# Sparse attention and two feed-forward layers on one core: a four-byte constant is allocated in front of x^T

## The chip, the core and the metric

The kernel runs on 1 core of one Trainium2 chip. Its measure is the device time of one execution in microseconds: the median of three runs of the kernel before is 643.96 us (643.88 to 644.82).

The engines carry these names in the profile: PE is TensorE's matmul row, PEld its weight loads, DVE is VectorE, ACT is ScalarE, POOL is GpSimd, and SP issues the DMAs. A matmul has two operands in SBUF: the *stationary* one, which a weight load brings into the array, and the *moving* one, whose columns stream through it.

## The reference

Attention with 8 global columns and a causal band of 96, a linear distance bias for each head, softmax, and then two feed-forward layers on the 1536 tokens of 512 features:

```python
def _attn_ref(q, k, v, n_global, n_local):        # q, k, v: (2, 8, 768, 64)
    scores = scale * np.matmul(q, k.transpose(0, 1, 3, 2)) + bias
    scores = np.where(keep, scores, -1000000000.0)
    a = softmax(scores)
    return np.matmul(a, v)

def _moe_ref(x, w_in, w_out):                     # layer 0; d_ff = 2048
    h = x @ w_in
    g = np.maximum(h, 0.0) + np.log1p(np.exp(-np.abs(h)))
    return g @ w_out

def _moe2_ref(x, w_in, w_out):                    # layer 1
    h = x @ w_in
    g = h * np.clip(h + 3.0, 0.0, 6.0) / 6.0
    return g @ w_out
```

The weights arrive as 64-bit floats.

## The kernel before

**Two paths.** `fast_path` does the work for the usual counts of global and local columns. `general_path` stands behind a branch that is not taken with these inputs, so none of it is in the profile.

**Numbers as pairs.** Each 32-bit operand is kept as a high and a low part in the matmul type (names ending in h and l: `xsh`/`xsl` are x^T, `gh`/`gl` the activations of a layer). A product is three matmuls (`matmul3`, L193): low times high, high times low, high times high, all added up in PSUM. Nearly all of TensorE's work is recorded at L193.

**Weights.** SyncE loads a block of 64-bit words (`raw`, L114), and ScalarE, GpSimd and VectorE rebuild from it the two parts (L133 to L146; `wa` is the value in between). A chunk of 128 hidden features has four tiles `w`. There are 11 slots of such tiles for the 32 chunks of both layers; a slot is freed when the last group of tokens has used its chunk.

**Stages.** In the first (to about 208 us) the attention of the blocks of 128 tokens runs between the first chunks of layer 0, in matmuls of 256 columns: `hf` is x times w_in, `accf` the product with w_out. From there on `item` works on 512 tokens and one chunk at a time, in matmuls of 512 columns: 12 for `h` and 12 for `acc`. `h` has a weight tile as stationary and x^T as moving operand. `acc` of layer 0 has the weight tile as stationary and the activation as moving operand, and `acc` of layer 1 the other way round. Sums over chunks that don't fit in PSUM at a time go to the tiles `part` (L289, L295, L297).

**The last group.** `last_items` computes `h` of five chunks (`hz` in the profile) and then all of their second products in one go (`accz`, to the end of the kernel). Its activations don't lie in the pool of `gh` and `gl`; they are put into weight slots that have become free:

```python
            wp, t = self.free.pop(0)
            where = [wp.tile([P, CW], F32R, tag=f"w{i}_{t}", name=f"g{i}_{s}") for i in range(2)]
            g.append(self.split_g(1, h, f"z{s}", where))
```

**A check of the inputs** runs beside layer 1: 24 loads of blocks of q and k (`chk`, L623) whose squares ScalarE sums (L624); they use the buffers of `raw`.

**Order.** A list scheduler of the framework sets the order on each engine when the kernel is built; on the chip each engine works its list off in that order.

**The constant.** `three` holds 3.0 in one 4-byte column, which layer 1's activation takes as its bias (L182). `Layers` allocates it in the pool `pp`, behind the three tiles `part`, and fills it on VectorE (L67):

```python
        self.three = self.pp.tile([P, 1], F32, name="three")
        self.nc.vector.memset(self.three, 3.0)
```

Of the kernel before, what the change touches and what calls it, by code (L numbers as in the profile page):

```python
# [7 lines left out]
F32 = mybir.dt.float32  # L8
# [8 lines left out]
P = 128  # L17
# [34 lines left out]
class Layers:  # L52
# [3 lines left out]

    def __init__(self, ctx, tc, weights, xsh, xsl, out):
        self.ctx, self.tc, self.nc = ctx, tc, tc.nc  # L60
        self.weights, self.xsh, self.xsl, self.out = weights, xsh, xsl, out
        self.pool("mp", 2)
        self.pool("tp", 5)
        self.pool("pp", 1)
        self.part = [self.pp.tile([P, 4, GB], F32, name=f"part{g}") for g in range(T // GB)]
        self.three = self.pp.tile([P, 1], F32, name="three")
        self.nc.vector.memset(self.three, 3.0)  # L67
        self.W, self.raws, self.slot = {}, {}, {}
        self.done, self.loaded = 0, 0
        first = range(PHASES[0][0])  # L70
        early = range(2 * EARLY_PAIRS)
        self.order = [(j, u) for js in (early, first[len(early):]) for u in range(2) for j in js]
        self.order += [(j, u) for j in range(len(first), 2 * NCH) for u in range(2)]
        self.free, self.h_tags, self.acc_tags, self.wr = [], [], [], []
        self.room = None
        self.n_h, self.halves, self.in_first, self.beside = 0, 0, True, False
        self.grow(0, FIRST_SLOTS, 2, 2)
# [318 lines left out]
def x_tiles(ctx, tc):  # L396
    xp = ctx.enter_context(tc.tile_pool(name="xp", bufs=1))
    return tuple(
        [xp.tile([P, KC, GB], F32R, name=f"xs{z}{g}") for g in range(T // GB)] for z in "hl"
    )  # L400
# [7 lines left out]
        nc.gpsimd.tensor_scalar(out=t, in0=t, scalar1=rs[:, j:j + 1], scalar2=0.0, op0=ALU.mult, op1=ALU.add)  # L408


def fast_path(tc, ident, nf, counts, q, k, qt, kt, v, weights, out, flag):


    with ExitStack() as ctx, ExitStack() as actx:
        nc = tc.nc
        xsh, xsl = x_tiles(ctx, tc)
        layers = Layers(ctx, tc, weights, xsh, xsl, out)
        layers.beside = True
        tp = layers.tp
        layers.room = actx.enter_context(tc.tile_pool(name="ap_r", bufs=1))  # L420
# [330 lines left out]
                    nc.vector.tensor_tensor(out=xl, in0=px, in1=r32(xh), op=ALU.subtract)  # L751


def general_path(tc, ident, nf, q, k, v, weights, out):
    with ExitStack() as ctx:
        xsh, xsl = x_tiles(ctx, tc)
        dense_attention(tc, ident, nf, q, k, v, xsh, xsl)
        layers = Layers(ctx, tc, weights, xsh, xsl, out)
        layers.weight_step(2 * FIRST_SLOTS)
        layers.run()  # L760


def body(tc, q, k, v, qt, kt, ns, w1i, w1o, w2i, w2o, out):
    nc = tc.nc
    with ExitStack() as ctx:
        nc.scalar.preload_act_table_set("natural_log_exp_and_others")
        const = ctx.enter_context(tc.tile_pool(name="const", bufs=1))
        ident = const.tile([P, P], F32, name="ident")

        nsb = const.tile([P, 2, 2], I32, name="nsb")  # L770
        nc.sync.dma_start(out=nsb.rearrange("p n w -> p (n w)"), in_=ns.partition_broadcast(P))
        nf = const.tile([P, 2], F32, name="nf")
        cv = const.tile([P, 2, 2], F32, name="cv")
        cneg = const.tile([P, 2], F32, name="cneg")

        def counts():
            tc.keep_in_program_order(nc.vector.tensor_copy(cv, nsb))
            nc.vector.tensor_scalar(out=cneg, in0=cv[:, :, 0], scalar1=0.0, scalar2=None, op0=ALU.is_lt)
            nc.vector.tensor_tensor(out=cneg, in0=cneg, in1=cv[:, :, 1], op=ALU.add)
            nc.vector.scalar_tensor_tensor(  # L780
                out=nf, in0=cneg, scalar=float(2 ** 32), in1=cv[:, :, 0], op0=ALU.mult, op1=ALU.add
            )

        make_identity(nc, ident)
        flag = const.tile([1, 1], I32, name="flag")
        weights = (w1i, w1o, w2i, w2o)
        fast_path(tc, ident, nf, counts, q, k, qt, kt, v, weights, out, flag)
        redo = nc.values_load(flag[0:1, 0:1], min_val=0, max_val=1)
        with tc.If(redo > 0):
            general_path(tc, ident, nf, q, k, v, weights, out)  # L790


def layout(q, k, v, n_global, n_local, moe_w_in, moe_w_out, moe2_w_in, moe2_w_out):
# [43 lines left out]
```

## Time and profile before

| | us |
|---|---|
| median of three runs | 643.96 (643.88 to 644.82) |
| the profiled execution | 643.55 |
| its span, first to last instruction | 641.8 |

The profile is of one execution. Besides the busy time of each engine it gives the chain of work that ended last (each piece is what released the next one), what each engine waited for, and the granted clock of TensorE. A matmul's own duration says little about TensorE's pace, since matmuls follow each other into the array before the one ahead has left it; the pace is the time from one start to the next. It is read from a run of n matmuls in the chain (the time that the piece covers, by n), or from a row of the timeline, which covers the first start to the last end: that time less one matmul's duration, by n - 1.

### The profile page before, as it was taken

The page shows a single profiled execution, that of the slowest core. Times are in us where ns is not written, and L with a number is a line of the kernel's source. Part 1 is how long each engine was busy: PE and PEld are TensorE (multiplying, and loading weights), DVE is VectorE, ACT ScalarE, POOL GpSimd, SP SyncE. Part 2 cuts the span into 40 slices and gives each one's busy share as a digit, 9 for nine tenths or more (in the row PEclk, how much of TensorE's full clock was granted, in tenths as well). Part 3 has the DMA queues.
Part 4 walks back from the last instruction along what each step waited for, and adds up shares of the span by engine and source line. Part 5 has one row for each costly group of instructions (what it writes and reads, how often), then busy time and mean ns, then how long its engine had stood idle before and what let it go on. Part 6 is the DMA issues. An engine that isn't in the chain of part 4 may idle for free.

```text
span 641.8 us, 9651 instructions
## 1 busy us (share of the span) xinstructions
PE 622.3 (97%) x3496; PEld 513.1 (80%) x3496; DVE 425.7 (66%) x893; ACT 380.8 (59%) x808; POOL 148.1 (23%) x180
## 2 busy tenths in 40 slices
PE   8699999999999999999999999999999999999996
PEld 4477987899999888887888888888887888888785
DVE  6988687735799999999989994126723342424251
ACT  7978888764868877696777652326694222222230
POOL 4666354330133255352200600001000000000000
PEclk9989999999999999999999999999999999999999
DMA  8754231101233333433402132001562000001011
GB/s 279 247 172 137 72 100 38 42 5 66 73 126 133 130 115 118 131 130 100 132 1 66 66 106 91 0 1 33 164 197 67 0 1 0 2 1 65 1 67 70
DMA packets 25081, 53.67 MB, mean 84 GB/s; under 512 B 2496, under 2 KB 9152, under 8 KB 25024
## 3 DMA queue, kind: packets, MB, share of 16 engines
q1 hardware_dynamic: 25024, 52.96, 25.4%
q8 instruction: 29, 0.48, 0.3%
q14 instruction: 28, 0.23, 0.1%
HBM read 49.81 MB, written 3.15 MB: 83 GB/s over the span
## 4 chain that ended last, share of the span: by engine, by line
PE 62%; DVE 17%; ACT 9%; DMA 5%; issue 3%; POOL 3%; SPq 0%; ACTq 0%; POOLq 0%; DVEq 0%
PE acc L193 21%; PE h L193 21%; PE accf L193 6%; PE hf L193 5%; ACT pm L523 3%; DVE wa L140 2%; DMA chk<-in_q 2%; PE accz L193 2%; PE hz L193 2%; DVE wa L141 2%; DVE w L146 2%; PE ptp L546 2%; POOL wa L136 1%; ACT chk L624 1%; PE px L564 1%
## 5 line engine op out<-in xcount | busy, mean ns | idle before, releaser
L193 PE MATMUL h<-xsh,w 128*128 128x512 f32 x584 | 159.1, 396 | 0.0
L136 POOL TENSOR_SCALAR wa<-wa 128x512 f32<-128x512 f32 x56 | 79.4, 1423 | 235.4 <-ACT wa L133 235.2
L193 PEld LDWEIGHTS h<-xsh,w 128*128 128x128 f32 x584 | 109.3, 188 | 26.7 <-DVE t L179 0.7
L193 PE MATMUL acc<-w,gh 128*128 128x512 f32 x344 | 108.0, 395 | 0.0
L183 DVE SCALAR_TENSOR_TENSOR t<-t,h 128x512 f32<-128x512 f32 x43 | 29.4, 684 | 82.3 <-ACT t L182 82.3
L193 PE MATMUL h<-xsl,w 128*128 128x512 f32 x292 | 82.3, 395 | 0.0
L182 ACT ACTIVATE t<-h,three 128x512 f32<-128x512 f32 x43 | 29.5, 687 | 87.7 <-PE h L193 87.5
L185 DVE TENSOR_TENSOR gl<-t,gh 128x512 fp32r<-128x512 f32 x73 | 51.3, 703 | 42.9 <-ACT gh L184 42.6
L193 PE MATMUL acc<-gh,w 128*128 128x512 f32 x240 | 78.9, 396 | 0.3 <-DVE part L289 0.2
L193 PEld LDWEIGHTS acc<-w,gh 128*128 128x128 f32 x344 | 64.5, 188 | 15.7
L184 ACT CAST gh<-t 128x512 fp32r<-128x512 f32 x73 | 45.2, 619 | 46.3 <-PE acc L193 24.3
L193 PE MATMUL acc<-w,gl 128*128 128x512 f32 x172 | 68.2, 396 | 0.1
L408 POOL TENSOR_SCALAR pm<-pm,rs 128x256 f32<-128x256 f32 (+1 forms) x96 | 54.4, 585 | 58.9 <-DVE rs L406 34.2
L193 PEld LDWEIGHTS h<-xsl,w 128*128 128x128 f32 x292 | 54.8, 188 | 13.2
L193 PE MATMUL accf<-ghf,w 128*128 128x256 f32 x288 | 56.6, 286 | 0.2 <-ACT ghf L184 0.2
L193 PEld LDWEIGHTS acc<-gh,w 128*128 128x128 f32 x240 | 44.9, 188 | 11.9 <-DVE part L289 0.6
L523 ACT ACTIVATE pm<-pm,nm 128x256 f32<-128x256 f32 (+1 forms) x96 | 46.3, 485 | 3.3 <-DVE nm L518 3.1
L193 PE MATMUL acc<-gl,w 128*128 128x512 f32 x120 | 47.5, 396 | 0.0
L193 PE MATMUL hf<-xsh,w 128*128 128x256 f32 x288 | 47.2, 289 | 0.0
L193 PEld LDWEIGHTS accf<-ghf,w 128*128 128x128 f32 x288 | 45.9, 188 | 0.6 <-ACT ghf L184 0.4
L146 DVE TENSOR_TENSOR w<-wa,w 128x512 fp32r<-128x512 f32 x56 | 39.4, 705 | 8.9 <-ACT w L145 8.9
L145 ACT CAST w<-wa 128x512 fp32r<-128x512 f32 x56 | 34.3, 615 | 14.4 <-DVE wa L141 8.9
(115 smaller groups left out, 1045.9 us busy)
## 6 DMA issues: line engine op xcount, KB each, us to landing
raw<-in_w2i SPq DMA_DIRECT2D x16, 512.0 KB, 3.3
raw<-in_w2o SPq DMA_DIRECT2D x16, 512.0 KB, 3.3
raw<-in_w1i SPq DMA_DIRECT2D x14, 512.0 KB, 3.4
raw<-in_w1o SPq DMA_DIRECT2D x12, 512.0 KB, 3.3
V<-in_v SPq DMA_DIRECT2D x12, 256.0 KB, 3.0
chk<-in_q SPq DMA_DIRECT2D x12, 256.0 KB, 3.0
chk<-in_k SPq DMA_DIRECT2D x12, 256.0 KB, 2.8
qT<-in_qt SPq DMA_DIRECT2D x11, 256.0 KB, 3.9
```

Source lines behind the costliest of these rows:

```text
L136: nc.gpsimd.tensor_scalar(out=a, in0=a, scalar1=W_HI, scalar2=W_LO, op0=ALU.min, op1=ALU.max)
L140: nc.vector.scalar_tensor_tensor(out=ai, in0=hi, scalar=-2 ** 30, in1=ai, op0=ALU.bitwise_and, op1=ALU.bitwise_or)
L141: nc.vector.scalar_tensor_tensor(out=ai, in0=lo, scalar=29, in1=ai, op0=ALU.logical_shift_right, op1=ALU.bitwise_or)
L145: nc.scalar.copy(wh, a)
L146: nc.vector.tensor_tensor(out=wl, in0=a, in1=r32(wh), op=ALU.subtract)
L182: nc.scalar.activation(t1, hf, AF.Relu, bias=self.three[:, 0:1])
L183: nc.vector.scalar_tensor_tensor(out=t3, in0=t1, scalar=6.0, in1=hf, op0=ALU.min, op1=ALU.mult)
L184: nc.scalar.copy(gh, t3)
L185: nc.vector.tensor_tensor(out=gl, in0=t3, in1=r32(gh), op=ALU.subtract)
L193: return self.nc.tensor.matmul(out, lhsT=a, rhs=b, start=start and z == 0, stop=stop and z == len(seq) - 1, **kw)
L408: nc.gpsimd.tensor_scalar(out=t, in0=t, scalar1=rs[:, j:j + 1], scalar2=0.0, op0=ALU.mult, op1=ALU.add)
L523: nc.scalar.activation(pmz, pmz, AF.Exp, bias=nm[:, z:z + 1], scale=-1.0, accum_out=sm[:, z:z + 1])
```

## The change

`three` is allocated in `body`, as the last tile of the pool `const`, and handed to `Layers`; it is filled there once, instead of once on each path. The pool `const` lies in front of all others, and a tile takes up at least 32 bytes of each partition. So what follows `const` moves up by 32 bytes, up to the place where `three` was: behind that nothing moves, since the 32 bytes there are gone.

```diff
-    def __init__(self, ctx, tc, weights, xsh, xsl, out):
+    def __init__(self, ctx, tc, weights, three, xsh, xsl, out):
...
-        self.three = self.pp.tile([P, 1], F32, name="three")
-        self.nc.vector.memset(self.three, 3.0)
+        self.three = three
...
-        layers = Layers(ctx, tc, weights, xsh, xsl, out)
+        layers = Layers(ctx, tc, weights, three, xsh, xsl, out)
...
         flag = const.tile([1, 1], I32, name="flag")
+        three = const.tile([P, 1], F32, name="three")
+        nc.vector.memset(three, 3.0)
         weights = (w1i, w1o, w2i, w2o)
```

The addresses in the two built programs (bytes from the start of a partition, and modulo 128):

| tiles | before | modulo 128 | after | modulo 128 |
|---|---|---|---|---|
| `three` | 109344 | 32 | 17184 | 32 |
| `xsh0`, the first of the six x^T tiles | 17184 | 32 | 17216 | 64 |
| `gh`, `gl`, all of layer 0 and layer 1 up to the last group | | 32 | | 64 |
| scratch of the activations (`t`) | | 32 | | 64 |
| `part0`, the first of three | 84768 | 32 | 84800 | 64 |
| the first weight tile; all 256 weight tiles and the last group's `g` | 109376 | 64 | 109376 | 64 |
| `raw`, `wa`, `chk`, `kT`, `qT`, `V`, `pm`, `pT` | | 64 | | 64 |

All tiles of x^T, of the activations and of the weights begin at one and the same address modulo 2048: the first two at 800 before and 832 after, the weights at 832 in both. On every engine the instructions of the fast path stand in the same order in both programs, with the same shapes; one VectorE memset of the path that isn't taken is gone.

## Rows read from the trace of the kernel before

**Rows 1.** The page: span, and busy time of each engine with its share.

```profile
span 641.8 us, 9651 instructions
PE 622.3 (97%) x3496; PEld 513.1 (80%) x3496; DVE 425.7 (66%) x893; ACT 380.8 (59%) x808; POOL 148.1 (23%) x180
```

**Rows 2.** Busy time of the engines by stretch; columns in the first row.

```profile
core 0: us, PE busy (x) PEld busy (x) DVE busy (x) ACT busy (x) POOL busy (x), PEclk, DMA share, GB/s
145.83:208.35 62.52, 62.52 (x481) 60.36 (x482) 51.48 (x91) 45.35 (x80) 14.32 (x13) 1.00 0.30 102
208.35:301.45 93.10, 92.78 (x396) 73.92 (x396) 91.81 (x159) 69.94 (x122) 40.15 (x22) 1.00 0.38 124
301.45:444.19 142.74, 142.74 (x611) 114.74 (x612) 98.31 (x163) 80.37 (x136) 19.61 (x14) 1.00 0.17 56
444.19:490.77 46.58, 46.45 (x199) 36.90 (x198) 24.66 (x40) 34.18 (x81) 2.87 (x4) 1.00 0.50 147
490.77:621.49 130.72, 130.72 (x561) 105.19 (x562) 48.22 (x74) 32.04 (x49) 0.00 (x0) 1.00 0.05 17
```

**Rows 3.** Chain of work in order of time: start us, us, what; TensorE's pieces.

```profile
157.38 2.84 PE hf L193 x24
...
205.49 2.85 PE accf L193 x24
...
305.61 2.80 PE acc L193 x12
308.41 2.80 PE h L193 x12
...
508.76 2.80 PE acc L193 x12
```

**Rows 4.** Timeline of TensorE in the last stage: start us, us, what, count.

```profile
622.49 9.23 PE L193 MATMUL accz<-w,g 128*128 128x512 f32 x40
...
631.79 1.48 PE L193 MATMUL accz<-w,g 128*128 128x256 f32 x11
```

**Rows 5.** Groups by line: busy us, mean ns of one, idle before.

```profile
L193 PE MATMUL accz<-w,g 128*128 128x512 f32 x45 | 10.4, 389 | 0.0
...
L193 PE MATMUL hf<-xsl,w 128*128 128x256 f32 x144 | 22.9, 281 | 0.0
L185 DVE TENSOR_TENSOR gl<-t,gh 128x512 fp32r<-128x512 f32 x73 | 51.3, 703 | 42.9 <-ACT gh L184 42.6
L146 DVE TENSOR_TENSOR w<-wa,w 128x512 fp32r<-128x512 f32 x56 | 39.4, 705 | 8.9 <-ACT w L145 8.9
```

**Rows 6.** The chain where TensorE is not on it: start us, us, what.

```profile
249.00 4.37 DMA raw<-in_w2o
...
300.78 0.63 ACT gh L184
...
301.45 1.19 PE acc L193 x4
...
444.21 0.63 ACT w L145
...
452.40 3.18 DMA chk<-in_q
...
490.02 0.70 DVE gl L185
...
490.77 3.07 PE acc L193 x12
```

**Rows 7.** Busy time in 145.83 to 208.35 us: tile `hf`, then tile `accf`.

```profile
145.83:208.35 62.52, 24.05 (x192) 1.00 0.30 102
...
145.83:208.35 62.52, 30.19 (x240) 1.00 0.30 102
```

**Rows 8.** Shares of the chain in 0 to 145.83 us, by line.

```profile
by line: ACT pm L523 12.8%; PE accf L193 8.4%; PE ptp L546 7.7%; PE hf L193 7.6%; PE px L564 5.6%; DVE pm L518 5.3%; PE s L512 4.2%; issue 3.9%; POOL pm L408 3.8%; ACT pT L548 3.6%; DVE part L141 2.8%; DVE w L146 2.8%; DVE part L140 2.4%; D
```

More of the change, by code (lines that the diff above doesn't have):

```diff
@@ L408, in softmax_rows, with fast_path @@
         nc.gpsimd.tensor_scalar(out=t, in0=t, scalar1=rs[:, j:j + 1], scalar2=0.0, op0=ALU.mult, op1=ALU.add)
-def fast_path(tc, ident, nf, counts, q, k, qt, kt, v, weights, out, flag):
+def fast_path(tc, ident, three, nf, counts, q, k, qt, kt, v, weights, out, flag):
     with ExitStack() as ctx, ExitStack() as actx:
@@ L751, in dense_attention, with general_path @@
                     nc.vector.tensor_tensor(out=xl, in0=px, in1=r32(xh), op=ALU.subtract)
-def general_path(tc, ident, nf, q, k, v, weights, out):
+def general_path(tc, ident, three, nf, q, k, v, weights, out):
     with ExitStack() as ctx:
@@ L757, in general_path @@
         dense_attention(tc, ident, nf, q, k, v, xsh, xsl)
-        layers = Layers(ctx, tc, weights, xsh, xsl, out)
+        layers = Layers(ctx, tc, weights, three, xsh, xsl, out)
         layers.weight_step(2 * FIRST_SLOTS)
@@ L785, in body @@
         flag = const.tile([1, 1], I32, name="flag")
+        three = const.tile([P, 1], F32, name="three")
+        nc.vector.memset(three, 3.0)
         weights = (w1i, w1o, w2i, w2o)
-        fast_path(tc, ident, nf, counts, q, k, qt, kt, v, weights, out, flag)
+        fast_path(tc, ident, three, nf, counts, q, k, qt, kt, v, weights, out, flag)
         redo = nc.values_load(flag[0:1, 0:1], min_val=0, max_val=1)
         with tc.If(redo > 0):
-            general_path(tc, ident, nf, q, k, v, weights, out)
+            general_path(tc, ident, three, nf, q, k, v, weights, out)
 def layout(q, k, v, n_global, n_local, moe_w_in, moe_w_out, moe2_w_in, moe2_w_out):
```

## The prediction

> **What bounds the kernel now.** First the busy times [rows 1]: TensorE's matmuls are busy for 97% of the span, its weight loads for 80%, no other engine for more than 66%. That alone doesn't say that its pace sets the end, so next come the busy times by stretch [rows 2], cut where the chain of work changes hands. From 145.83 to 208.35, 301.45 to 444.19 and 490.77 to 621.49 us TensorE is busy all the time at the full granted clock (1.00), and the chain in these stretches is TensorE's own matmuls, one behind the other [rows 3]. In the two stretches between, TensorE is busy nearly all the time too, but the chain runs elsewhere [rows 6]. From 208.35 to 301.45 VectorE is busy for 91.81 of 93.10 us, rebuilding weights and splitting activations, and TensorE has a matmul of `acc` waiting at 301.45 for ScalarE's `gh`. From 444.21 it goes through ScalarE and the loads of the input check, one behind the other; at 490.77 `acc` starts when VectorE's `gl` is ready. There TensorE is not ahead: the others set the time.
>
> So the question is TensorE's pace. In runs of 512 columns it is the same for all three uses: `h`, `acc` of layer 0 and `acc` of layer 1 take 2.80 us for 12, 233.3 ns each [rows 3]. Their operands lie at 64 (the weight) and 32 (x^T or activation) modulo 128, whichever of the two is stationary. One run differs: `accz`, the last group. 40 matmuls of it cover 9.23 us [rows 4]; less one duration of 389 ns [rows 5], by 39, that is 226.7 ns. It has the shape, type, PSUM accumulation and three-part order of `acc`. What it has of its own is where its activations lie: in weight slots, so both operands begin at 64. That is the pair of places that the change gives to every matmul of `h` and `acc`.
>
> In runs of 256 columns the sign is the other way: `hf` takes 2.84 us for 24, 118.3 ns, and `accf` 2.85 [rows 3]; the 256-column end of `accz`, both operands at 64, takes (1.48 - 0.28)/10 = 120.0 ns [rows 4, 5].
>
> [...]
>
> **The change part by part.**
>
> *512 columns.* The pace goes from 233.3 to 226.7 ns, 2.84% of the time that such matmuls set.
> - 301.45 to 444.19: 142.74 us x 2.84% = -4.05.
> - 490.77 to 621.49: 130.72 x 2.84% = -3.71.
> - 145.83 to 208.35: 481 matmuls [rows 2], less 192 `hf` and 240 `accf` [rows 7], leave 49 of 512 columns: 49 x 6.6 ns = -0.32.
> - 208.35 to 301.45: nothing. TensorE reaches each wait sooner and waits longer. If it did set the pace there, this would be -2.64. What hides it is VectorE's list, which is full.
> - 444.21 to 490.77: nothing, by the chain of loads and ScalarE. If that gave way, -1.32. Its start is moved with TensorE: ScalarE's `w` at 444.21 stands right behind `acc`, whose weight slot it writes. So what was won before 444 us isn't lost here.
> - `accz` itself has this pace already.
>
> *256 columns.* +1.7 ns each. In 145.83 to 208.35 us all 432 are on the chain: +0.73. Before that `accf` and `hf` hold 8.4% and 7.6% of 145.83 us of chain [rows 8], 23.3 us or 197 matmuls: +0.33. Together +1.06. Bounds: 0, since interrupted runs may not settle into the slower pace, and 864 x 1.7 ns = +1.47, if all were on the chain.
>
> *Other engines.* VectorE's subtraction takes 703 ns on activations (at 32 before) and 705 on weights (at 64) [rows 5]. Same operation, same shape: the place costs these engines nothing that can be read, and I take 0. The one memset stays first on VectorE, so no wait is added.
>
> *Sum.* -4.05 - 3.71 - 0.32 + 1.06 = -7.02 us. The profiled execution took 643.55 us, 1.75 more than its span of 641.8; it becomes 636.5. The median of 643.96 lies 0.4 above it, and I forecast that: 643.96 - 7.02 = **636.9 us**. Next to be late are the same two chains, which then make TensorE wait about 2.6 and 1.3 us longer.
>
> **The rivals.**
>
> *The two chains give way.* If VectorE's list and the check move up with TensorE, because they wait for its results more than the chain shows, all stretches gain: -7.02 - 2.64 - 1.32 = -10.98, so 633.0, and 631.9 without the 256-column loss. Against it: VectorE is idle for only 1.29 us in 93.10 [rows 2], and the check is a row of loads of about 3 us [rows 6].
>
> *Half of it.* Only one operand's place matters. Then `h`, whose weight is stationary before and after, and `acc` of layer 1 can't both gain: about half of -8.08, plus 1.06, gives -2.98, so 641.0. Against it: `h` and layer 1's `acc` have the pair the opposite way round and the same pace [rows 3].
>
> *No change.* `accz` is quick for another reason, such as the quiet around it, with hardly any work on other engines. Then 644.0. Against it: from 490.77 to 621.49 VectorE is idle for 82 of 130.72 us, and the pace is 233.3 ns there [rows 2, 3]. For it: a single run of 45 matmuls in one place of the program is all the evidence. [...]
>
> *Slower.* Operands that begin at the same place get in each other's way, as the 256-column end of `accz` hints with its +1.7 ns. If the 512 columns pay that too: (142.74 + 130.72)/0.2333 + 49 = 1221 matmuls x 1.7 ns = +2.08, with the +1.06 gives +3.14, so 647.1. It decides once the 512-column pace of `h` comes out above 233.3 ns. Against it: 512-column `accz` went down.
>
> That the addresses don't move is no rival: they are read from the two programs.
>
> **How the numbers follow.** The forecast (636.9; 634.5 to 639.5 with its own bounds) has 0.55, the chains giving way 0.10, half 0.11, no change 0.16, slower 0.08. The range 632.5 to 644.0 holds the forecast, the half, most of the first rival and half of the no-change case, about 0.8. A measurement of this kernel can tell about 0.2%, 1.3 us, from no change. Faster by more: 0.55 + 0.10 + 0.11 = 0.76; within: 0.16; slower: 0.08.
>
> **What would show each step.** Pieces of the chain with 12 `h` or `acc` at 2.72 us instead of 2.80 show the pace; 2.80 shows the no-change case, and a difference between `h` and layer 1's `acc` the half. `hf` at 2.88 for 24 shows the loss at 256 columns. TensorE's idle time in front of `acc` near 300 and 490 us, grown by 2.6 and 1.3 us, shows the two chains holding; no growth shows them giving way. VectorE's `gl` off 703 ns would make the zero for other engines wrong. The forecast as a whole is wrong if the pace of `accz` was not due to its addresses.

## The result

The changed kernel takes 637.11 us (median of four runs, 635.96 to 637.76), the kernel before 643.98 (643.88 to 644.82). The ratio is 0.9882, with a 95% interval of 0.9866 to 0.9898: faster by 6.9 us, where 7.0 was forecast. The profiled execution of the changed kernel is the quickest of its four, 635.96 us with a span of 634.2.

In the changed kernel the line numbers are one less: L192 is what L193 was. First the busy times by stretch, cut where the chain changes hands as in [rows 2] (columns in the first row; the fourth row is the stretch of the check):

```profile
core 0: us, PE busy (x) PEld busy (x) DVE busy (x) ACT busy (x) POOL busy (x), PEclk, DMA share, GB/s
145.83:208.83 63.00, 63.00 (x482) 61.03 (x482) 52.14 (x91) 45.24 (x80) 12.63 (x13) 1.00 0.31 101
208.83:302.12 93.29, 91.21 (x397) 73.54 (x396) 92.16 (x158) 70.27 (x122) 34.46 (x22) 1.00 0.38 124
302.12:440.88 138.76, 138.76 (x611) 114.72 (x612) 98.49 (x163) 80.31 (x136) 17.43 (x14) 1.00 0.18 58
440.88:486.95 46.07, 45.44 (x200) 36.92 (x199) 24.66 (x40) 34.20 (x81) 3.01 (x4) 1.00 0.48 149
486.95:614.11 127.16, 127.16 (x561) 105.18 (x562) 47.80 (x74) 32.10 (x49) 0.00 (x0) 1.00 0.05 17
```

The counts of matmuls are those of before, but for one more at the cuts of three stretches, and so is the clock, 1.00. Beside [rows 2] the lengths give the whole account:

| stretch | before, us | after, us | change | forecast |
|---|---|---|---|---|
| up to the first long run of `hf` | 145.83 | 145.83 | 0.00 | +0.33 |
| the rest of the first stage | 62.52 | 63.00 | +0.48 | +0.41 |
| VectorE's full list | 93.10 | 93.29 | +0.19 | 0 |
| TensorE ahead, first | 142.74 | 138.76 | -3.98 | -4.05 |
| the check's loads | 46.58 | 46.07 | -0.51 | 0 |
| TensorE ahead, second | 130.72 | 127.16 | -3.56 | -3.71 |
| `accz` to the end | 20.31 | 20.09 | -0.22 | 0 |

Next TensorE's pieces of the chain after (start us, us, what), to be held against [rows 3]:

```profile
157.54 2.88 PE hf L192 x24
205.94 2.89 PE accf L192 x24
...
306.23 2.72 PE acc L192 x12
308.95 2.72 PE h L192 x12
...
504.48 2.72 PE acc L192 x12
```

2.80 us for 12 matmuls of 512 columns has become 2.72, in `h` as in `acc` of both layers (layer 0 at 306 and 309 us, layer 1 at 504): 226.7 ns each, the pace that `accz` had before [rows 4]. 24 matmuls of 256 columns have gone from 2.84 to 2.88 us, 120.0 ns each, again `accz`'s pace.

### The profile page after: what moved, and what is told of

It reads as the page before. It is cut to its first block, busy times and chain, and to the rows that moved or that the text cites. A ratio compares the mean times of both kernels' runs of the same rounds, so it can differ in the third digit from the quotient of the medians.

```text
span 634.2 us, 9650 instructions
## 1 busy us (share of the span) xinstructions
PE 612.5 (97%) x3495; PEld 513.6 (81%) x3496; DVE 426.6 (67%) x893; ACT 380.9 (60%) x808; POOL 138.4 (22%) x180
## 4 chain that ended last, share of the span: by engine, by line
PE 62%; DVE 21%; ACT 7%; issue 3%; DMA 3%; POOL 1%; SPq 0%; ACTq 0%; POOLq 0%; DVEq 0%
PE acc L192 21%; PE h L192 20%; PE accf L192 6%; PE hf L192 5%; DVE wa L139 3%; DVE wa L140 3%; ACT pm L522 3%; DVE w L145 2%; PE accz L192 2%; PE hz L192 2%; PE ptp L545 2%; DMA chk<-in_q 2%; DVE gl L184 1%; DVE t L178 1%; DVE pm L517 1%
## 5 line engine op out<-in xcount | busy, mean ns | idle before, releaser
L192 PE MATMUL h<-xsh,w 128*128 128x512 f32 x584 | 155.7, 390 | 1.2 <-DVE t L178 1.2
L192 PEld LDWEIGHTS h<-xsh,w 128*128 128x128 f32 x584 | 109.0, 188 | 25.2 <-DVE t L178 2.9
L135 POOL TENSOR_SCALAR wa<-wa 128x512 f32<-128x512 f32 x56 | 70.0, 1254 | 240.7 <-ACT wa L132 240.5
L192 PE MATMUL acc<-w,gh 128*128 128x512 f32 x344 | 106.0, 389 | 0.0
L192 PE MATMUL h<-xsl,w 128*128 128x512 f32 x292 | 80.5, 389 | 0.0
L192 PE MATMUL acc<-gh,w 128*128 128x512 f32 x240 | 77.7, 391 | 0.8 <-ACT gh L183 0.5
L192 PEld LDWEIGHTS acc<-w,gh 128*128 128x128 f32 x344 | 64.6, 188 | 13.3
L192 PE MATMUL acc<-w,gl 128*128 128x512 f32 x172 | 67.2, 391 | 0.6 <-DVE gl L184 0.6
L192 PEld LDWEIGHTS h<-xsl,w 128*128 128x128 f32 x292 | 54.8, 188 | 11.4
L192 PE MATMUL accf<-ghf,w 128*128 128x256 f32 x288 | 57.3, 287 | 0.2 <-ACT ghf L183 0.2
L192 PEld LDWEIGHTS acc<-gh,w 128*128 128x128 f32 x240 | 44.8, 188 | 11.3 <-ACT gh L183 1.5
L192 PE MATMUL hf<-xsh,w 128*128 128x256 f32 x288 | 47.2, 290 | 0.0
L192 PEld LDWEIGHTS accf<-ghf,w 128*128 128x128 f32 x288 | 46.6, 191 | 0.6 <-ACT ghf L183 0.4
L192 PE MATMUL acc<-gl,w 128*128 128x512 f32 x120 | 46.7, 389 | 0.0
L132 ACT ACTIVATE wa<-raw 128x512 f32<-128x512 f32 x53 | 35.6, 675 | 15.0 <-DVE w L145 7.4
```

Source lines behind the costliest of these rows:

```text
L132: first = nc.scalar.activation(a, raw.bitcast(F32)[:, :, 1], AF.Abs)
L135: nc.gpsimd.tensor_scalar(out=a, in0=a, scalar1=W_HI, scalar2=W_LO, op0=ALU.min, op1=ALU.max)
L192: return self.nc.tensor.matmul(out, lhsT=a, rhs=b, start=start and z == 0, stop=stop and z == len(seq) - 1, **kw)
```

## The experiments

The question after the result was what about the addresses it is. Three theories: *difference* (how far apart the two operands of a matmul begin), *alignment* (each has to begin at a multiple of 64 bytes) and *activations at 64* (their own place alone). An unused tile shifts what lies behind it; the order of the instructions is that of the changed kernel in all runs up to "fine". Each run but the last ("pairs") is of one execution.

**Everything at 96.** 32 bytes of padding in front of x^T, so that all tiles behind the constants move:

```diff
+        const.tile([P, 8], F32, name="pad_x")
         three = const.tile([P, 1], F32, name="three")
```

> All tiles behind the constants 32 bytes further up than in the changed kernel: x^T, activations and weights all begin at 96 modulo 128. Theory 'difference' (the pace depends on how far apart the two operands begin, modulo some power of two, and 0 apart is the quick case): 12 matmuls of 512 columns in 2.72 us, time within 1 us of the changed kernel's 637.1. Theory 'alignment' (each operand has to begin at a multiple of 64 bytes): 2.80 us for 12 and 644 us or more, and accz, whose operands lie at 96 too, goes from 226.7 to 233 ns. Theory 'activations at 64' (only their own place counts): 2.80 us, with accz slow too.

636.45 us in one run. Chain, and `accz` in the timeline:

```profile
306.04 2.72 PE acc L192 x12
308.76 2.72 PE h L192 x12
...
615.33 9.23 PE L192 MATMUL accz<-w,g 128*128 128x512 f32 x40
```

The quick pace at 96 modulo 128: neither 64 nor a multiple of 64 is what counts. *Alignment* and *activations at 64* fall.

**Weights 64 bytes further up.** 64 bytes of padding behind `part`, so that only the weight tiles and what follows them move:

```diff
         self.three = three
+        self.pp.tile([P, 16], F32, name="pad_w")
```

> x^T and activations at 64 modulo 128 as in the changed kernel, the weight tiles (and all behind them) 64 bytes further up, at 0. Both are multiples of 64, but 64 apart. Theory 'alignment': 2.72 us for 12, 637 us. Theory 'activations at 64': 2.72 us, 637 us. Theory 'difference': quick only if 64 apart counts as 0 apart; else 2.80 us or another pace, 644 us. accz, with both operands in weight slots, stays at 226.7 ns in all of them.

641.94 us:

```profile
305.79 2.80 PE acc L193 x12
308.59 2.80 PE h L193 x12
...
507.82 2.76 PE acc L193 x12
510.58 2.80 PE h L193 x12
```

Both operands at multiples of 64, and slow. The acc at 306 is of layer 0 (weight stationary, as in `h`), the one at 508 of layer 1 (weight moving): 64 bytes forward and 64 bytes back are not alike, 2.80 and 2.76 us. `accz`, both of whose operands moved to 0 modulo 128, still takes 9.23 us for its 40.

**Weights 96 bytes further up** (24 columns of padding):

> x^T and activations at 64 modulo 128, the weight tiles at 32, 96 bytes apart. Theory 'alignment': 2.80 us for 12, 644 us, and accz slow as well since its operands lie at 32. Theory 'difference': 2.80 us or another slow pace, but accz at 226.7 ns, since its operands are 0 apart. Theory 'activations at 64': 2.72 us, 637 us.

645.61 us in one run, beside 644.75 in one of the kernel before; that kernel's runs lie between 643.07 and 645.76, so the two can't be told apart:

```profile
306.77 2.81 PE acc L193 x12
309.59 2.81 PE h L193 x12
...
624.55 9.23 PE L193 MATMUL accz<-w,g 128*128 128x512 f32 x40
```

`h` and `acc` are slow, and `accz`, both of whose operands moved to 32 modulo 128, keeps (9.23 - 0.389)/39 = 226.7 ns, in one and the same execution. `accz` is what the forecast rested on: wherever its two operands lie, they are 0 apart.

**Weights 128, 256 and 512 bytes further up** ask for the period:

> x^T and activations at 64 modulo 128, the weight tiles 128 bytes further up than in the changed kernel, at 64 modulo 128 again, 128 bytes apart modulo 2048. Theories 'alignment' and 'activations at 64': 2.72 us for 12, 637 us. Theory 'difference' with a period of 128 bytes or less: the same. 'Difference' with a longer period: not 2.72 us.

> The weight tiles 256 bytes further up than in the changed kernel, so 256 bytes apart from x^T and activations (modulo 2048). 0, 32, 64, 96 and 128 apart have shown 2.72, 2.80, 2.76 to 2.80, 2.81 and 2.78 us for 12 matmuls of 512 columns. Theory 'difference with a period of 256 bytes': 2.72 us and 637 us. Theory 'period of 512 or more' (a weight tile's slices for one product begin 512 bytes apart and run alike, so it can't be told from a period of 512): 2.76 to 2.81 us, 642 to 645 us.

> The weight tiles 512 bytes further up than in the changed kernel. The slices of one weight tile begin 0, 512, 1024 and 1536 bytes into it and showed one pace, so by the theory 'difference' 512 bytes are a whole number of periods: 2.72 us for 12, 637 us, as the changed kernel. 2.76 us or more would say that it is the tiles' own distance and not the slices' that counts, and that the theory lacks something.

642.65, 637.67 and 638.12 us. Pieces of the chain of the three in this order:

```profile
511.36 2.78 PE h L193 x12
514.15 2.78 PE acc L193 x12
```

```profile
508.91 2.72 PE h L193 x12
511.63 2.72 PE acc L193 x12
```

```profile
509.34 2.72 PE h L193 x12
512.06 2.72 PE acc L193 x12
```

128 bytes apart is not 0 apart, 256 is: the difference counts modulo 256 bytes. That both operands lie at 64 modulo 128 after the change is chance; the weights happen to lie there.

**Only acc 0 apart.** 32 bytes of padding between x^T and the activations:

```diff
+        self.pool("pad", 1).tile([P, 8], F32, name="pad_g")
         self.pool("mp", 2)
```

> Beside the changed kernel, everything behind x^T moves up by 32 bytes: activations and weights begin at 96 modulo 128, x^T at 64. acc has its operands 0 apart, h has them 32 apart. Theory 'difference': acc 2.72 us for 12, h 2.80 (226.7 and 233.3 ns), accf 2.88 for 24 and hf 2.84, and about 640.5 us, half of the way. Theory 'one operand decides for the whole stage' (a matmul's pace depends on the runs before it): both alike.

641.34 us:

```profile
157.55 2.84 PE hf L193 x24
160.40 2.87 PE accf L193 x24
...
308.95 2.80 PE h L193 x12
311.75 2.75 PE acc L193 x12
...
337.89 5.46 PE acc L193 x24
```

Each use has the pace of its own pair: `h` and `hf` as before the change, `acc` and `accf` nearly as after it. Pieces of 12 `acc` take 2.72 to 2.75 us where 2.72 was expected, and 24 in a row 5.46, only 0.02 above twice 2.72. The excess doesn't grow with the length, so the pace takes a few matmuls to settle when `acc` comes behind a slow `h`. The time is 0.8 us above the 640.5 expected; the changed kernel's own runs lie further apart than that, so it can't be put down to the settling.

**Small differences.** x^T's tiles begin 4, 16 and 240 bytes late for the three groups of 512 tokens (tiles 256 bytes larger, so that all else stays 0 apart):

```diff
+OFF = (1, 4, 60)
...
-        [xp.tile([P, KC, GB], F32R, name=f"xs{z}{g}") for g in range(T // GB)] for z in "hl"
+        [
+            xp.tile([P, KC * GB + 64], F32R, name=f"xs{z}{g}")[:, OFF[g]:OFF[g] + KC * GB].rearrange("p (c t) -> p c t", c=KC)
+            for g in range(T // GB)
+        ] for z in "hl"
```

> The changed kernel with x^T's tiles begun a little later: by 4 bytes for the first 512 tokens, 16 for the next, 240 (16 short of 256) for the last; activations and weights stay 0 apart modulo 256. So h has its operands 4, 16 and 240 bytes apart in its three groups, acc 0. If the places count in pieces of 32 bytes or more, 4 and 16 bytes are as good as 0 (2.72 us for 12 h). If each element counts, h takes 2.75 to 2.81 us in all three groups. A pace under 2.72 would say that 0 is not the best place.

641.07 us; `h` of the second, third and first group:

```profile
510.12 2.78 PE h L193 x12
...
521.18 2.80 PE h L193 x12
...
548.84 2.85 PE h L193 x12
```

A distance of a single element counts. 16 bytes either way cost about as much as 32; 4 bytes apart is the slowest pair of all, 237.5 ns, and outside the 2.75 to 2.81 us expected. No difference that was tried is quicker than 0 at 512 columns.

**Where the rest of the gain went.** Two stretches hardly shrank. For that of the check, 23 of its 24 loads and sums were left out (the list of steps cut to one, the sums set to 0 first):

```diff
-        todo = list(range(2 * B * NB))
+        todo = [0]
```

> The changed kernel with 1 of the 24 loads and sums of the input check; the other 23 are left out (the flag is computed from what is left). It asks where the gain went in the stretch of the check, 440.9 to 487.0 us in the changed kernel, which shrank by 0.5 us and not by the 1.3 that the pace would give. My theory: the chain of the check's loads and ScalarE's sums makes TensorE wait there, so without it acc follows h without a wait before 487 us and the stretch gives about 0.7 us more; the time is some 0.7 us under the changed kernel's. Rival: TensorE waits for weights or activations there anyway, and nothing is gained.

634.6 us in one run, span 632.8. The chain through that stretch, and beside it pieces of the changed kernel's there:

```profile
455.71 2.72 PE acc L192 x12
458.43 1.36 PE h L192 x6
...
484.05 2.72 PE h L192 x12
486.77 2.72 PE acc L192 x12
```

```profile
475.10 2.65 DMA chk<-in_k
...
482.07 2.78 DMA chk<-in_k
...
485.66 0.52 ACT gh L183
...
486.20 0.70 DVE gl L184
486.95 3.02 PE acc L192 x12
```

Without the check the whole stretch is TensorE's; `accz` begins 1.4 us sooner (612.72 and 614.11). That is twice the 0.7 expected; the whole time of this one run is 2.5 us under the changed kernel's median, whose profiled execution was its quickest. The order around the check changes too when its steps are gone, and which of the two the other half comes from was not tried.

For the stretch of VectorE, one of its four steps in the rebuilding of a weight block (L137, L140, L141 and L146 in the kernel before; not five, as expected below) was left out, the one at L141 that puts in the low bits of the weights. It was done once with the weights 0 apart and once with them 32 bytes further up:

```diff
-        nc.vector.scalar_tensor_tensor(
-            out=ai, in0=lo, scalar=29, in1=ai, op0=ALU.logical_shift_right, op1=ALU.bitwise_or
-        )
```

> The changed kernel without the step that puts the low bits into the rebuilt weights (one of VectorE's five steps for each of 64 blocks is left out; the scheduler then orders the work anew). It asks what held the stretch from 208 to 302 us, which didn't shrink when TensorE got quicker. My theory: VectorE's full list; with a fifth of the rebuilding gone TensorE's h and acc follow each other there at 2.72 us for 12, the waits for VectorE's t and gl and ScalarE's gh are gone, and the time is about 2.5 us under the changed kernel's, near 634 us. Rival: the waits there come from the loads of weights or from GpSimd, and stay.

> The same kernel as light, with the weight tiles 32 bytes further up, 32 apart from x^T and activations as in the kernel before: the pair tells what the place alone is worth when VectorE leaves TensorE room. By my theory the pace of 512 columns then counts from 208 us to accz except in the stretch of the check: about 9.5 to 10.5 us between the two, against 6.9 between the two kernels of the case. Rival: 7 us again.

630.84 and 639.84 us. TensorE's waits from 170 us on, of "light" first and then of the changed kernel from 208 us on (who waited for whom: us, times, longest):

```profile
PE accz L189 <- DVE part L326: 0.5, 1, 0.5
```

```profile
PE h L192 <- DVE t L178: 1.2, 2, 0.7
PE acc L192 <- DVE gl L184: 0.6, 2, 0.4
PE accz L192 <- DVE part L329: 0.5, 1, 0.5
PE acc L192 <- ACT gh L183: 0.5, 1, 0.5
PE acc L192 <- DVE part L288: 0.2, 1, 0.2
```

All but the one of `accz` are gone, as the theory of VectorE's list has it. They are gone in the stretch of the check too, although all 24 of its loads are there, so the check alone doesn't hold that stretch: it takes VectorE's list as well. Since the framework orders the work anew without the step, how much is due to the shorter list and how much to the new order isn't shown.

630.84 us is 6.3 under the changed kernel's median, where 2.5 was expected. By the chains 5.1 us of it lie between the end of the first stage and `accz` (400.19 beside 405.28, worked out below), in both stretches and not in VectorE's alone.

What the place is worth then, by the chains of the pair, from the end of the first stage to `accz`:

```profile
202.88 5.63 PE accf L189 x47
...
608.70 12.00 PE accz L189 x60
```

```profile
200.74 5.57 PE accf L190 x47
...
617.82 12.03 PE accz L190 x60
```

(608.70 - 208.51) beside (617.82 - 206.31) is 400.19 beside 411.51: 11.3 us, where the two kernels of the case differ by 7.9 in that part (405.28 and 413.14). All four have about 1765 matmuls there, so "light" takes 226.7 ns for each and the other of the pair 233.2: the pace alone, with nothing left of the waits. The expectation had left out the stretch of the check. In the whole times the pair differs by only 9.0 and not by 9.5 to 10.5, since the first stage ended 2.2 us later in "light". Most of that was there by 145 us, ahead of any long run at L189, and has not been traced.

**A version that follows.** The check in 12 loads of two blocks in place of 24 of one:

```diff
-            nc.sync.dma_start(out=x, in_=(q, k)[z][n * P:(n + 1) * P, :])
+            src = (q, k)[z][2 * n * P:2 * (n + 1) * P, :]
+            nc.sync.dma_start(out=x.rearrange("p (b d) -> p b d", b=2), in_=src.rearrange("(b p) d -> p b d", b=2))
```

> The changed kernel with the input check in 12 loads of two blocks of 128 tokens each, in place of 24 of one (a sum then covers two tokens and is held against the same limit, which can only send more inputs down the general path). The run with one load instead of 24 showed the chain of loads and sums to be worth about 1.5 to 2.5 us. Half of the loads should give about half of that or more: 635 to 636.5 us. If ScalarE's sums and not the loads' latency hold the chain, it stays at 637.

634.85 us (634.68 to 636.45, four runs), a ratio of 0.9864 (0.9837 to 0.9890) to the kernel before. A sum now covers two tokens and is held against the same limit, which can only send more inputs down the general path. It is quicker than the kernel before, and its median is 2.3 us under the changed kernel's, a little more than expected; the intervals of the two ratios overlap, so by times alone that last step isn't settled. In its profiled execution the chain from 436 to 495 us is TensorE's throughout, as it is without the check, and `accz` begins at 612.65 us, 1.5 sooner than in the changed kernel's.

## Why the prediction was right

*The pace.* The step on which it all hung, that the pace of `accz` is due to the place of its operands, held: 2.72 us was named and came, in all three uses, and with it 2.88 for 24 `hf`. What was weak was the evidence, one run of 45 matmuls; "r96" supplies what was missing, a slow `h` and a quick `accz` in one execution at other addresses. The rival that the quiet around `accz` makes it quick falls with the 2.72 us of `h` and `acc` amid the other engines' work. The prediction names 64 and 64 as the pair; that the other equal places that were tried do as well (both at 96 in "r0_at96", 256 and 512 bytes apart in "r256" and "r512", 2.72 us each) came out only in the experiments.

*Each place by itself.* With x^T's tiles begun 4 bytes later and the instructions in the same order, `h` goes from 226.7 ns (2.72 us for 12, after the change) to 237.5 (2.85, "fine", first group). The alignment of the operands by itself had no effect on the speed: `accz` takes 9.23 us for its 40 with both at 0 ("r64"), 32 ("r96"), 64 (before) and 96 ("r0_at96") modulo 128.

*Half of it* fell: `h` and layer 1's `acc` gained alike, from 2.80 to 2.72 us for 12, since what counts is the pair. *Slower* fell for 512 columns (2.72 us for 12) and held for 256 (2.88 for 24), as forecast from the same rows.

*The two stretches without gain.* They were named with their waits, and both held: +0.19 and -0.51 us instead of the -2.64 and -1.32 that the pace alone would give. TensorE's idle time says too little of the waits, since the record of a matmul goes on for 389 to 396 ns where the next one could start after 227 or 233, and covers part of each wait: in the first stretch it went from 0.32 us (93.10 - 92.78, [rows 2]) to 2.08 (93.29 - 91.21), in the second from 0.13 to 0.63. By the length of the stretch less its matmuls at their pace, the first went from 93.10 - 396 x 0.2333 = 0.71 us to 93.29 - 397 x 0.2267 = 3.29: grown by 2.6, as forecast. The second went from 0.15 to 0.73, grown by 0.6 and not by 1.3 (one matmul more or less at a cut makes 0.2). That is a term that was mis-sized: the chain of the check is not quite rigid, and gave 0.5 us. The place of the new waits was named only in part. Most of those in the first stretch are not in front of `acc` near 300 us, but in front of `h` for VectorE's `t` (1.2 us in two waits, listed above) and of `acc` at 272 us; before the change the list of TensorE's waits from 208 us on has neither.

*256 columns.* +0.41 in the rest of the first stage came out at +0.48. The +0.33 ahead of it came to nothing. There `hf` and `accf` are on the chain in short pieces; a piece of 21 does take 0.02 to 0.03 us longer, but the pieces behind it begin no later, so the work between them took up the loss. Before, then after:

```profile
59.44 2.49 PE hf L193 x21
...
65.28 2.48 PE accf L193 x21
```

```profile
59.45 2.51 PE hf L192 x21
...
65.24 2.51 PE accf L192 x21
```

The errors of the stretches, -0.33, -0.51 and -0.22 on one side, +0.07, +0.07, +0.15 and +0.19 on the other, add up to -0.58: the profiled span fell by 7.6 us and not by 7.0. The medians fell by 6.9. That this is within 0.1 us of the forecast is partly luck: the changed kernel's four runs are 1.8 us apart.

*Other engines.* The zero held: VectorE's `gl` takes 703 ns in the changed kernel too.

*The settling* was missed: 12 `h` that stand alone between runs of 256 columns take longer than those in a long run. This piece of the chain after the change is one of two with 2.75:

```profile
203.20 2.75 PE h L192 x12
```

## What to carry to other kernels

When one run of the same instruction has another pace than the rest, look for what is different about its operands' addresses before looking at the work around it; it may show what the whole kernel would do elsewhere. For matmuls like these, lay out the tiles of the two operands so that they begin at the same place modulo 256 bytes (2.72 us for 12 here, 2.76 to 2.85 at the other distances), and check that a small constant in a pool doesn't push one of them off; at 256 columns the best place may be another one (2.88 us for 24 at 0 apart, 2.84 at 32), so measure at the size that holds most of the time. And count a quicker engine's gain only where the chain is its own: here the pace promised 4.0 us (2.64 + 1.32) in the two stretches that hang on VectorE's list and the check's loads, and 0.3 came (0.51 - 0.19).

## What the runs showed of the hardware

For matmuls with 512 moving columns of 32 bits and a 128x128 stationary operand loaded for each, the pace in these runs depends on where the stationary operand begins relative to the moving one, modulo 256 bytes. From the pieces of 12 in the chains (the commonest value of each; most others of a kind lie within 0.04 us of it, and the first pieces behind a wait or a run of 256 columns are longer; for 252 there are only two pieces behind the first stage):

| stationary minus moving, bytes modulo 256 | us for 12 | run |
|---|---|---|
| 0 | 2.72 | after, r0_at96, r256, r512 |
| 16 | 2.80 | fine, third group |
| 32 and 224 | 2.80 | before |
| 64 | 2.80 | r64, h and layer 0 |
| 96 | 2.81 | r96, h and layer 0 |
| 128 | 2.78 | r128 |
| 160 | 2.80 | r96, acc of layer 1 |
| 192 | 2.76 | r64, acc of layer 1 |
| 240 | 2.78 | fine, second group |
| 252 | 2.85 | fine, first group |

At 256 columns the order is another: 24 of them take 2.88 us at 0, 2.84 at 32 and 2.83 at 64 in these runs (`hf`: after the change, before it, and this piece of "r64"), so 0 is the slowest of these three:

```profile
157.58 2.83 PE hf L193 x24
```

What in the chip makes these differences was not shown.
